# Clustered attention and two feed-forward layers: the first head pair's clusters chosen head by head, the second pair's preparation moved into the first ticks

## The chip, the cores and the metric

One core of a Trainium2 chip runs one program. Its engines work from queues of their own: TensorE (PE, with its weight loads shown as PEld), VectorE (DVE), ScalarE (ACT), GpSimd (POOL) and SyncE (SP), which only issues transfers here. The metric is the device time of one execution in microseconds, as the median of several runs. Lower is better.

## What is computed

Sixteen attention problems (2 batches by 8 heads, 768 tokens, 64 dimensions each) in which a query sees only the keys of its own cluster, then two feed-forward layers over all 1536 tokens:

```
q_assign = argmax(einsum('bhsd,hcd->bhsc', q_n, c_n))      # 16 clusters a head; q_n, k_n, c_n normalised
k_assign = argmax(einsum('bhsd,hcd->bhsc', k_n, c_n))
scores = where(q_assign[..., None] == k_assign[..., None, :], scale * q @ k.T, -1e9)
attn = softmax(scores) @ v
h = x @ w_in;  g = max(h, 0) + alpha * min(h, 0);  y = g @ w_out        # layer 1
h = y @ w_in2; g = max(h, 0) + log1p(exp(-abs(h))); out = g @ w_out2    # layer 2
```

Every product is done in split precision: an operand is stored as a high part (rounded to fp32r) and a low part (the rest), and the products of the parts are summed.

## The kernel before, in words

Attention goes by pairs of heads, eight pairs in all (`pairs`). The work on one pair is cut into named steps (`steps_of`). For its preparation they are, by name and line: `hik`/`hiq` high parts on ACT (L369, L372), `lok` low part of the keys on POOL (L383), `lq` low part of the queries on DVE (L388, two halves), `sq` squares (on ACT for the first two pairs, L329, on POOL for the others, L331), `fold` six halving additions of the squares on POOL (L348), `inv0` to `inv2` the inverse norms (Ln and Exp on ACT L131/L132, then `inv1`: a reciprocal on DVE L135 and two POOL additions, then `inv2`: a POOL scaling L139 and the reciprocal `rinv` on DVE L140), `dk`/`dq`/`dh`/`dl` the products with the centroids on PE (L403, tile `dps`), `de` their copies on ACT (L411), `dt` their transposes on PE (L428).

Choosing a cluster is then: `dn` = `dt` times `rinv` (DVE L442), `mx` its maximum over 16 clusters, `eq` comparison with the maximum and multiplication with a falling `rank`, `m2` the maximum again, and `oh` the one-hot row. For the first pair all six operations are on DVE and work on both heads, queries and keys at once (128x384 elements, L442 to L476), and `dn` stands in PSUM, in one of the two buffers that later hold scores. For other pairs some are on POOL, and `dn` stands in SBUF. The one-hot rows are transposed on PE (`ot`, L492) and become the mask rows: `rq` (ACT, L507) and `rk` (DVE, L511) write those of the first head straight into its operands `mq` and `mk`; `mr` (ACT, L500) writes a copy from which `mk1` sends the second head's by DMA.

The attention itself runs in 96 ticks, one for 128 queries of one head, 12 to a pair. In tick u stand, in this order: `scores(u)` (PE, four matmuls, tile `s`, L599/L600; two buffers), `exps(u-1)` (ACT L614, tile `e`), `maxima(u)` (DVE, tile `nm`, L605), steps due at phase E, `transposes(u-2)` (PE, tile `pt`, L627), `highs`/`lows` (ACT `ph` L643, DVE `pl` L647), `attend(u-4)` (PE, tile `o`), and steps due at phase L. The whole attention is under a manual schedule: each engine executes in the order in which the code is run, and stands still where its next instruction has to wait.

What is run before tick 0 is the list `PRELUDE`. Later steps stand in tables (`FIRST`, `SECOND`, `THIRD`, `STEADY`, `LAST`): a number x of pair n means tick (n-2)*12 + ceil(x), phase L for a whole number, else E. So in `SECOND` 12 is tick 0 and 15.5 is tick 4, phase E; in `FIRST` 24 is tick 0; in `THIRD` 3 is tick 3. `warm(n)` is n transposes of the identity on PE whose result (`wps`) nobody reads.

Before the change, `PRELUDE` holds also the second pair's squares, folds and low parts (`sq0 1`, `fold0 1`, `lq0 1`), and the second pair's `dn` and `mx` stand at 13.5 and 14, that is in tick 2.

## Time and profile before

| what | value |
|---|---|
| time, median of 3 runs | 807.17 us (806.46 to 807.91) |
| the profiled execution: span from first to last instruction | 804.5 us |
| what lies around that span in a run, by the difference | 2.7 us |
| busy share of the span: PE, DVE, ACT, POOL | 97%, 73%, 62%, 44% |
| mean granted TensorE clock, as a share of 2.4 GHz | 0.987 |
| first maximum of scores (`nm` of tick 0) starts at | 21.72 us |
| `nm` of tick 2, 5, 6 starts at | 28.60, 35.90, 39.55 us |

The opening is some 45 of 804.5 us. A microsecond in it counts in full where PE stays busy from there on. Times in rows are microseconds from the span's start.

### The profile page before, as it was taken

The page shows a single profiled execution, that of the slowest core. Times are in us where ns is not written, and L with a number is a line of the kernel's source. Part 1 is how long each engine was busy: PE and PEld are TensorE (multiplying, and loading weights), DVE is VectorE, ACT ScalarE, POOL GpSimd, SP SyncE. Part 2 cuts the span into 40 slices and gives each one's busy share as a digit, 9 for nine tenths or more (in the row PEclk, how much of TensorE's full clock was granted, in tenths as well). Part 3 has the DMA queues.
Part 4 walks back from the last instruction along what each step waited for, and adds up shares of the span by engine and source line. Part 5 has one row for each costly group of instructions (what it writes and reads, how often), then busy time and mean ns, then how long its engine had stood idle before and what let it go on. Part 6 is the DMA issues. An engine that isn't in the chain of part 4 may idle for free.

```text
span 804.5 us, 11964 instructions
## 1 busy us (share of the span) xinstructions
PE 780.4 (97%) x4139; PEld 666.7 (83%) x4139; DVE 585.3 (73%) x923; ACT 496.0 (62%) x1024; POOL 356.8 (44%) x380
## 2 busy tenths in 40 slices
PE   6899999999998979999999999999999999999998
PEld 6789999999997758888888888888888888888886
DVE  7689989989989977547646835978469569765444
ACT  5788999999999778346536535674366245343221
POOL 6567668778354775026115404585144036023000
PEclk9899999999999989999999999999999999999999
DMA  9666667655552343102302401312014012000002
GB/s 265 180 166 172 152 170 173 182 145 128 119 144 64 105 157 132 53 26 79 105 0 72 138 1 53 132 53 78 1 53 156 2 53 81 24 2 1 28 31 97
DMA packets 26955, 75.91 MB, mean 94 GB/s; under 512 B 4464, under 2 KB 7408, under 8 KB 26896
## 3 DMA queue, kind: packets, MB, share of 16 engines
q1 hardware_dynamic: 26896, 75.16, 32.3%
q8 instruction: 32, 0.52, 0.3%
q14 instruction: 27, 0.22, 0.1%
HBM read 49.36 MB, written 3.15 MB: 65 GB/s over the span
## 4 chain that ended last, share of the span: by engine, by line
PE 78%; DVE 11%; ACT 3%; POOL 3%; issue 3%; DMA 1%; SPq 0%; DVEq 0%; POOLq 0%; ACTq 0%
PE acc L935 29%; PE hp L876 27%; PE pt L627 6%; PE o L657 6%; PE s L599 3%; PE s L600 3%; DVE r L173 2%; DVE pl L647 2%; POOL t L178 1%; DVE nm L605 1%; PE dps L403 1%; DVE m L168 1%; DVE y L950 1%; DVE lo L388 1%; ACT e L614 1%
## 5 line engine op out<-in xcount | busy, mean ns | idle before, releaser
L876 PE MATMUL hp<-xh,ih 128*128 128x512 f32 x384 | 150.2, 392 | 1.3 <-ACT e L614 1.3
L876 PE MATMUL hp<-xl,ih 128*128 128x512 f32 x384 | 150.1, 391 | 0.0
L876 PE MATMUL hp<-xh,il 128*128 128x512 f32 x384 | 149.9, 391 | 0.0
L181 POOL TENSOR_TENSOR il<-t,ih 128x512 fp32r<-128x512 f32 x32 | 44.3, 1385 | 198.7 <-ACT ih L180 188.3
L917 DVE TENSOR_TENSOR gl<-hp,gh 128x512 fp32r<-128x512 f32 x96 | 65.9, 686 | 69.6 <-ACT gh L916 69.5
L916 ACT CAST gh<-hp 128x512 fp32r<-128x512 f32 x96 | 56.4, 587 | 88.8 <-PE acc L935 69.9
L605 DVE TENSOR_REDUCE nm<-s 128x1 f32<-128x768 f32 x96 | 90.9, 947 | 18.3 <-PE s L600 18.3
L647 DVE TENSOR_TENSOR pl<-pt,ph 128x384 fp32r<-128x384 f32 x192 | 97.3, 548 | 5.8 <-ACT ph L643 4.9
L178 POOL TENSOR_TENSOR t<-m,r 128x512 uint32<-128x512 uint32 x64 | 85.6, 1337 | 30.8 <-DVE r L173 16.3
L643 ACT CAST ph<-pt 128x384 fp32r<-128x384 f32 x192 | 84.0, 485 | 14.7 <-PE pt L627 14.1
L614 ACT ACTIVATE e<-s,nm 128x768 f32<-128x768 f32 x96 | 87.9, 916 | 3.0 <-DVE nm L605 2.4
L898 ACT ACTIVATE sp<-a 128x512 f32<-128x512 f32 x48 | 30.4, 632 | 92.5 <-DVE a L894 92.5
L627 PE MATMUL pt<-ident,e 128*128 128x128 f32 x576 | 83.2, 277 | 4.1 <-DVE pl L647 4.0
L876 PEld LDWEIGHTS hp<-xh,ih 128*128 128x128 f32 x384 | 72.4, 189 | 16.5 <-ACT e L614 1.6
L876 PEld LDWEIGHTS hp<-xh,il 128*128 128x128 f32 x384 | 72.5, 189 | 15.2
L876 PEld LDWEIGHTS hp<-xl,ih 128*128 128x128 f32 x384 | 72.4, 189 | 15.1
L627 PEld LDWEIGHTS pt<-ident,e 128*128 128x128 f32 x576 | 66.9, 141 | 16.4 <-DVE pl L647 13.0
L935 PE MATMUL acc<-gh,oh 128*128 128x512 f32 x192 | 72.6, 395 | 5.4 <-ACT gh L916 5.4
L935 PE MATMUL acc<-gl,oh 128*128 128x512 f32 x192 | 75.7, 394 | 0.2 <-DVE gl L917 0.2
L935 PE MATMUL acc<-gh,ol 128*128 128x512 f32 x192 | 75.2, 392 | 0.0
L935 PE MATMUL acc<-ol,gh 128*128 128x512 f32 x192 | 74.7, 389 | 0.0
L935 PE MATMUL acc<-oh,gh 128*128 128x512 f32 x192 | 74.7, 389 | 0.0
(171 smaller groups left out, 1671.8 us busy)
## 6 DMA issues: line engine op xcount, KB each, us to landing
raw<-in_w_in_dram SPq DMA_DIRECT2D x32, 512.0 KB, 3.3
raw<-in_w_out_dram SPq DMA_DIRECT2D x32, 512.0 KB, 3.3
tok<-in_qk_tok_dram SPq DMA_DIRECT2D x8, 768.0 KB, 6.1
ak<-hi SPq DMA_DIRECT2D x31, 192.0 KB, 3.0
...
```

The source lines that it names most:

```text
L178: nc.gpsimd.tensor_tensor(out=t.bitcast(U32), in0=mu, in1=r, op=ALU.add)
L181: nc.gpsimd.tensor_tensor(out=low, in0=t, in1=high.bitcast(F32), op=ALU.subtract)
L605: nc.vector.tensor_reduce(out=nm, in_=st[u]["s"][:, :, 0:HS], axis=AX.XY, op=ALU.max, negate=True)
L614: nc.scalar.activation(out=e.rearrange("p (a j) c -> p a (j c)", a=2), in_=st[u]["s"][:, :, 0:HS], func=AF.Exp, bias=st[u]["nm"], scale=1. ...
L627: nc.tensor.transpose(pt[:, j * P : (j + 1) * P], st[u]["e"][:, 3 * a + j, :], ident)
L643: nc.scalar.copy(out=dh, in_=src)
L647: nc.vector.tensor_tensor(out=dl, in0=src, in1=dh.bitcast(F32), op=ALU.subtract)
L657: nc.tensor.matmul(acc[key][:, 0:QG], lhsT=vv[:, j, 2 * hh : 2 * hh + 2, :].rearrange("p a d -> p (a d)"), rhs=grp[key][part][:, j, :], st ...
L876: nc.tensor.matmul(hp, lhsT=a_[:, cs], rhs=b_[:, c, ts], start=n == 0, stop=n == 3 * NC_ - 1)
L916: nc.scalar.copy(out=gh, in_=hp)
L917: nc.vector.tensor_tensor(out=gl, in0=hp, in1=gh.bitcast(F32), op=ALU.subtract)
L935: nc.tensor.matmul(accs[c], lhsT=a_, rhs=b_, start=opens and n == 0, stop=closes and n == 2)
```

## The change

The six operations of the choice become a function `choose(hh, parts)` that works on one head (128x192 elements, every other group of 16), and a pair's two heads are chosen apart:

```
+                    q["oh"] = ap1.tile([P, J, 4 * C], F32R, tag="oh", name="oh")
+                    nc.gpsimd.memset(q["oh"].bitcast(F32).rearrange("p j (s h c) -> p j s h c", s=2, h=2)[:, :, :, 1], 0.0)
+                    return
...
+            def choose(hh, parts):
+                one = [P, n_ // 2, C]
+                dn, mx, m2 = q["dn"][:, hh::2], q["mx"][:, hh::2], q["m2"][:, hh::2]
+                oh = q["oh"].rearrange("p j (n c) -> p (j n) c", c=C)[:, hh::2]
+                r_ = rank[:, None, :].to_broadcast(one)
+                if 0 in parts:
+                    nc.vector.tensor_tensor(
+                        out=dn,
+                        in0=q["dt"][:, 0 : n_ * C].rearrange("p (n c) -> p n c", c=C)[:, hh::2],
+                        in1=q["rinv"][:, hh::2, None].to_broadcast(one),
+                        op=ALU.mult,
+                    )
+                if 1 in parts:
+                    nc.vector.tensor_reduce(out=mx, in_=dn, axis=AX.X, op=ALU.max)
+                if 2 in parts:
+                    nc.vector.tensor_tensor(out=dn, in0=dn, in1=mx[:, :, None].to_broadcast(one), op=ALU.is_equal)
+                if 3 in parts:
+                    nc.vector.tensor_tensor(out=dn, in0=dn, in1=r_, op=ALU.mult)
+                if 4 in parts:
+                    nc.vector.tensor_reduce(out=m2, in_=dn, axis=AX.X, op=ALU.max)
+                if 5 in parts:
+                    nc.vector.tensor_tensor(out=oh, in0=dn, in1=m2[:, :, None].to_broadcast(one), op=ALU.is_equal)
...
-            def onehot(t):
-                if first_:
+            def onehot(t, near=False):
+                if near:
                     q["ot", t] = ps_t.tile([P, 512], F32R, tag="t", name="ot")
...
+                st_[f"on{t}"] = lambda t=t: onehot(t, True)
...
 PRELUDE = [
-    "hik0 0", "hik1 0", "lok 0", "hiq0 0", "hiq1 0", "warm 18", "centroids_high", "centroids_low", "lq0 0",
+    "hik0 0", "hik1 0", "lok 0", "centroids_high", "centroids_low", "hiq0 0", "hiq1 0", "warm 8", "lq0 0",
...
+    "lok 1", "hiq0 1", "hiq1 1", "warm 17", "dn 0", "ch0 0", "on0 0", "on1 0",
+    "dh0 1", "dh1 1", "op1a 0", "op1b 0", "op1c 0", "minus_alpha",
+    "rq0 0", "rk0 0", "rk1 0", "rq1 0", "ch10 0", "ch11 0", "go 0", "ld 1", "lt 1",
...
 FIRST = dict(
-    va0=24, va1=26, lv=26.5,
+    ch12=23.5, ch13=23.5, ch14=24, ch15=24, on0=25, on1=25, mr0=25, mr1=25.5, mk1=25.5, va0=24, va1=27, lv=27.5,
```

`ch0` is the first head's whole choice; `ch10` to `ch15` are the six operations of the second head's. The second head's one-hot columns are first set to zero by POOL, since the transposes `on0`/`on1` of the prelude read both heads' columns. They are run a second time in tick 1, when the second head is chosen. In `SECOND` the second pair's `sq0=12, sq1=12, lq0=12.5, lq1=13, fold0=13, fold1=13.5, fold2=14` are new, and `inv0` moves from 12 to 14, `inv1` from 12.5 to 15, `inv2` from 13 to 15.5, `dt` from 13 to 14, `dn` from 13.5 to 15.5, `mx` from 14 to 16, `eq` from 16 to 17, `m2` from 18 to 18.5. The warming transposes are 18, 8, 9 and 17 ahead of tick 0 (before: 18, 18 and 14).

What stands on DVE between the first pair's one-hot row and the seventh maximum, before (from tick 0 to tick 4; `mk` is `rk`, `nm` a maximum, `lo` is `lq`, the second and later `dn` and `mx` are the second pair's):

```order
L388 SCALAR_TENSOR_TENSOR lo<-dim,hi 128x384 x2
L511 TENSOR_SCALAR mk<-ot,mscale,mbias_96 16x384 x2
L605 TENSOR_REDUCE nm<-s 128x1 x2
L135 RECIPROCAL s_383<-s_367 128x24
L140 RECIPROCAL rinv<-s_383 128x24
L605 TENSOR_REDUCE nm<-s 128x1
L442 TENSOR_TENSOR dn<-dt,rinv 128x384
L647 TENSOR_TENSOR pl<-pt,ph 128x3x128 x2
L454 TENSOR_REDUCE mx<-dn 128x24
L605 TENSOR_REDUCE nm<-s 128x1
L647 TENSOR_TENSOR pl<-pt,ph 128x3x128 x2
L605 TENSOR_REDUCE nm<-s 128x1
```

The same place after the change, from the second maximum on (ahead of it stand the two `mk`, two operations of the second head's choice, the first `nm` and the other four):

```order
L626 TENSOR_REDUCE nm<-s 128x1
L387 SCALAR_TENSOR_TENSOR lo<-dim,hi 128x384 x2
L626 TENSOR_REDUCE nm<-s 128x1
L668 TENSOR_TENSOR pl<-pt,ph 128x3x128 x2
L626 TENSOR_REDUCE nm<-s 128x1
L668 TENSOR_TENSOR pl<-pt,ph 128x3x128 x2
L134 RECIPROCAL s_471<-s_436 128x24
L626 TENSOR_REDUCE nm<-s 128x1
L139 RECIPROCAL rinv<-s_471 128x24
L445 TENSOR_TENSOR dn<-dt,rinv 128x384
L668 TENSOR_TENSOR pl<-pt,ph 128x3x128 x2
L485 TENSOR_REDUCE mx<-dn 128x24
```

The two `lo` moved from ahead of the mask rows to between the maxima of ticks 1 and 2, and the two reciprocals, `dn` and `mx` of the second pair moved from ticks 1 and 2 to ticks 3 and 4, ahead of that tick's `pl`.

PE at the start of the ticks, before (rows from the first pair's one-hot transposes to the third unit's scores, with the queues whose signal each waits for):

```order
L492 MATMUL ot<-identr,oh 64x128 [waits DVE_49,PE_49]
L492 MATMUL ot<-identr,oh 64x128 x2
L492 MATMUL ot<-identr,oh 64x128 [waits PE_49]
L492 MATMUL ot<-identr,oh 64x128 x2
L599 MATMUL s<-ak,aq 128x384 [waits DMAHW1_49,DMAHW2_49,DMAHW0_49,Pool_49]
L600 MATMUL s<-mk,mq 128x384 [waits DVE_49,Pool_49]
L599 MATMUL s<-ak,aq 128x384
L600 MATMUL s<-mk,mq 128x384
L403 MATMUL dps<-lo,chz 64x384 [waits Pool_49]
L403 MATMUL dps<-lo,chz 64x384 x3
```

and after, from the same transposes on:

```order
L512 MATMUL ot<-identr,oh 64x128 [waits DVE_49,PE_49,Pool_49]
L512 MATMUL ot<-identr,oh 64x128 x2
L512 MATMUL ot<-identr,oh 64x128 [waits DVE_49]
L512 MATMUL ot<-identr,oh 64x128 x2
L402 MATMUL dps<-hi,chz 64x384
```

and, from the second unit's scores (ahead of them stand eight `dps<-hi` and the first unit's four) to the eight warming transposes:

```order
L620 MATMUL s<-ak,aq 128x384 [waits Activation_49]
L621 MATMUL s<-mk,mq 128x384
L620 MATMUL s<-ak,aq 128x384
L621 MATMUL s<-mk,mq 128x384
L512 MATMUL ot<-identr,oh 64x128 [waits DVE_49]
L512 MATMUL ot<-identr,oh 64x128 x5
L402 MATMUL dps<-lo,chz 64x384
L402 MATMUL dps<-lo,chz 64x384 [waits DVE_49]
L402 MATMUL dps<-lo,chz 64x384
L402 MATMUL dps<-lo,chz 64x384 [waits DVE_49]
L211 MATMUL wps<-ident 128x128 [waits Activation_49]
L211 MATMUL wps<-ident 128x128 x7
```

The second half's first transposes now wait for DVE: `dt` still holds one of the two buffers that they turn in, so both halves use the other, and `rk0` must have read the first. The second unit's scores wait for ACT: `dn` still holds one of the two buffers of the scores, so the first unit's `exps` must have read the other. The four `dps<-lo` products, the eight `wps` and the third unit's scores stand behind the two `lo` of DVE.

POOL in ticks 2 to 4, before:

```order
L565 TENSOR_TENSOR vv<-rawv,vv 128x6x64
L136 TENSOR_TENSOR s_383<-sq,s_383 128x24
L137 TENSOR_TENSOR s_383<-s_383,s_367 128x24
L139 TENSOR_SCALAR s_383<-s_383 128x24
L564 CAST vv<-rawv 128x6x64
```

and after:

```order
L586 TENSOR_TENSOR vv<-rawv,vv 128x6x64
L135 TENSOR_TENSOR s_471<-sq,s_471 128x24
L136 TENSOR_TENSOR s_471<-s_471,s_436 128x24
L330 TENSOR_TENSOR sq<-tok 128x768
L138 TENSOR_SCALAR s_471<-s_471 128x24
L486 TENSOR_TENSOR dn<-dn,mx 128x384
L382 TENSOR_TENSOR lo<-dim,hi 128x768
```

The third pair's squares (`sq<-tok`, `THIRD` has them in tick 3) now stand between the second and the third of the operations that make the second pair's inverse norm.

## Rows read from the trace of the kernel before

**Rows 1.** The page's first part: busy time and share of each engine.

```profile
PE 780.4 (97%) x4139; PEld 666.7 (83%) x4139; DVE 585.3 (73%) x923; ACT 496.0 (62%) x1024; POOL 356.8 (44%) x380
```

**Rows 2.** Three windows: length, then each engine's busy time (count), granted clock, DMA.

```profile
22.00:28.00 6.00, 5.55 (x24) 4.83 (x23) 2.24 (x4) 3.28 (x9) 3.00 (x6) 0.50 0.59 170
...
30.00:45.00 15.00, 13.08 (x89) 11.25 (x89) 13.06 (x23) 12.44 (x30) 8.75 (x7) 1.00 0.88 214
45.00:55.00 10.00, 10.00 (x83) 9.65 (x82) 8.12 (x13) 8.95 (x22) 6.85 (x11) 1.00 0.56 126
```

**Rows 3.** Timeline to 17 us: start, length, engine, line, tile, [idle before <-releaser].

```profile
7.75 1.58 ACT L329 ACTIVATE sq<-tok 128x768 f32<-128x768 f32 x2 [0.84 <-DMA tok<-in_qk_tok_dram]
...
12.69 0.57 DVE L442 TENSOR_TENSOR dn<-dt,rinv 128x384 f32<-128x384 f32 x1
...
13.69 1.82 POOL L383 TENSOR_TENSOR lo<-dim,hi 128x768 fp32r<-128x768 f32 x1 [4.06 <-ACT hi L369]
...
15.22 0.42 PE L403 MATMUL dps<-hi,chz 128*64 128x384 f32 x1
...
15.68 0.56 DVE L476 TENSOR_TENSOR oh<-dn,m 128x384 fp32r<-128x384 f32 x1
```

**Rows 4.** Groups to 60 us, shapes apart: total busy, mean ns, idle before.

```profile
L276 POOL MEMSET clz<- 128x384 f32 x1 | 0.4, 432 | 0.0
...
L261 DVE TENSOR_TENSOR csq<-cexp 128x128 f32<-128x128 f32 x1 | 0.3, 293 | 0.6 <-DMA cexp<-in_centroids_dram 0.6
```

**Rows 5.** Timeline 15.9 to 25 us: from the first one-hot row to the second maximum.

```profile
15.95 3.98 POOL L348 TENSOR_TENSOR sq<-sq 128x768 f32<-128x768 f32 x3 [0.43 <-ACT sq L329]
...
16.16 3.32 DVE L388 SCALAR_TENSOR_TENSOR lo<-dim,hi 128x384 fp32r<-128x384 f32 x2
...
16.70 0.53 PE L492 MATMUL ot<-identr,oh 128*64 128x128 f32 x6
...
17.08 0.66 ACT L507 ACTIVATE mq<-ot,mbias,mscale 16x384 fp32r<-16x384 f32 x1 [1.21 <-PE ot L492]
...
19.51 1.26 DVE L511 TENSOR_SCALAR mk<-ot,mscale,mbias 16x384 fp32r<-16x384 f32 x2
...
20.92 0.41 PE L600 MATMUL s<-mk,mq 80*128 80x384 f32 x1 [3.47 <-DVE mk L511]
...
21.72 0.96 DVE L605 TENSOR_REDUCE nm<-s 128x1 f32<-128x768 f32 x1 [0.94 <-PE s L600]
...
22.71 0.90 ACT L614 ACTIVATE e<-s,nm 128x768 f32<-128x768 f32 x1
...
24.07 0.96 DVE L605 TENSOR_REDUCE nm<-s 128x1 f32<-128x768 f32 x1 [1.40 <-PE s L600]
```

**Rows 6.** Timeline 25 to 42 us: ticks 2 to 6 (maxima of ticks 2, 5, 6).

```profile
25.32 1.97 PE L212 MATMUL wps<-ident 128*128 128x128 f32 x8
...
26.93 0.67 PE L599 MATMUL s<-ak,aq 128*128 128x384 f32 x1
...
28.60 0.96 DVE L605 TENSOR_REDUCE nm<-s 128x1 f32<-128x768 f32 x1 [1.97 <-PE s L600]
...
35.13 0.85 DVE L465 SCALAR_TENSOR_TENSOR dn<-dn,rank 128x384 f32<-128x384 f32 x1
...
35.90 0.94 DVE L605 TENSOR_REDUCE nm<-s 128x1 f32<-128x768 f32 x1
...
37.70 0.54 DVE L388 SCALAR_TENSOR_TENSOR lo<-dim,hi 128x384 fp32r<-128x384 f32 x1
...
39.55 0.96 DVE L605 TENSOR_REDUCE nm<-s 128x1 f32<-128x768 f32 x1 [1.31 <-PE s L600]
```

**Rows 7.** Timeline at 58 us: the third pair's inverse norm.

```profile
58.20 0.30 DVE L140 RECIPROCAL rinv<-s 128x24 f32<-128x24 f32 x1 [1.50 <-POOL s L139]
```

**Rows 8.** Groups to 60 us, shapes apart: POOL squares and ACT Ln.

```profile
L331 POOL TENSOR_TENSOR sq<-tok 128x768 f32<-128x768 f32 x3 | 4.7, 1569 | 0.1
...
L131 ACT ACTIVATE s<-sq,tiny 128x24 f32<-128x24 f32 x2 | 0.7, 338 | 0.0
```

More of the change, by code (lines that the diff above doesn't have):

```diff
@@ L447, in _ @@
                 )
+            def choose(hh, parts):
[20 more added lines that the diff above has]
+                    nc.vector.tensor_tensor(out=oh, in0=dn, in1=m2[:, :, None].to_broadcast(one), op=ALU.is_equal)
+            for hh in range(2):
+                for part in range(6):
+                    st_[f"ch{hh}{part}"] = lambda hh=hh, part=part: choose(hh, [part])
+                st_[f"ch{hh}"] = lambda hh=hh: choose(hh, range(6))
             @step("mx")
@@ L454, in _ @@
                 nc.vector.tensor_reduce(out=q["mx"], in_=dn, axis=AX.X, op=ALU.max)
-                if not first_:
-                    nc.gpsimd.tensor_tensor(out=dn, in0=dn, in1=q["mx"][:, :, None].to_broadcast(every), op=ALU.subtract)
+                nc.gpsimd.tensor_tensor(out=dn, in0=dn, in1=q["mx"][:, :, None].to_broadcast(every), op=ALU.subtract)
             @step("eq")
@@ L460, in _ @@
                 dn, r_ = q["dn"], rank[:, None, :].to_broadcast(every)
-                if first_:
-                    nc.vector.tensor_tensor(out=dn, in0=dn, in1=q["mx"][:, :, None].to_broadcast(every), op=ALU.is_equal)
-                    nc.vector.tensor_tensor(out=dn, in0=dn, in1=r_, op=ALU.mult)
-                else:
-                    nc.vector.scalar_tensor_tensor(
-                        out=dn, in0=dn, scalar=0.0, in1=r_, op0=ALU.is_equal, op1=ALU.mult
-                    )
+                nc.vector.scalar_tensor_tensor(
+                    out=dn, in0=dn, scalar=0.0, in1=r_, op0=ALU.is_equal, op1=ALU.mult
+                )
             @step("m2")
```

18 lines of the change are left out of this document (6 added, 12 removed), and 6 rows, old and new, of the table PRELUDE.

## The prediction

> **What bounds the kernel now.** Read first the shares by engine: PE is busy 97% of the span [rows 1], so outside the opening the time is PE's, and what the opening loses or gains is carried to the end. Then the windows. From 22 to 28 us PE's granted clock is 0.50, the lower of its two levels (1.2 GHz), and from 30 to 45 us it is 1.00, but DVE is busy 13.06 of 15 us and PE is not full [rows 2]: here DVE is the engine that sets the ticks. From 45 to 55 us PE is busy without a gap [rows 2]. Then the timeline. The first one-hot row is done at 16.24 (15.68 + 0.56) [rows 3], but DVE next runs the second pair's two `lo` for 3.32 us, until 19.48, and only then the mask rows `mk` for 1.26 us; PE stands 3.47 us for them, and the first maximum starts at 21.72, the second at 24.07 [rows 5]. The third waits for PE until 28.60: eight warming transposes of 0.2 us (25.32 to 26.93) and four products stand ahead of it. The maxima of ticks 5 and 6 are at 35.90 and 39.55 [rows 6].
>
> The change takes the two `lo` out of the first wait and halves the choice. It also puts new waits in, and DVE work into ticks that DVE sets. I walk through it, with the start of `nm` in each tick as the mark, in us against before.
>
> **1. Choice and memset (to the first transposes): -1.0.** The six operations stand 0.60 apart (12.69 to 15.68 is five of them) [rows 3]. Half width lies between 0.29 for 128 elements [rows 4] and 0.57 for 384 [rows 3], on a line 0.36, so 0.39 apart: six take 2.3. They begin where they did, since the squares wait for their load at 7.75 [rows 3], which nothing moves; at best 0.3 sooner, as the centroid copy goes ahead; I take 0.2. So DVE is done at 14.8. But the transposes read both heads' columns and wait for POOL's memset, behind POOL's `lo`, which ends at 15.51 [rows 3]. Half of a memset that took 0.43 [rows 4] is 0.25, so 15.5 to 15.7. On PE stand 17 warming transposes from 12.4; at 0.2 each [rows 6] they end at 15.8, less if the clock rises. I take 15.7 instead of 16.70 [rows 5].
>
> **2. Mask rows and first scores: -0.75 more.** From transposes to `rq` was 0.38, `rq` 0.66, each `mk` 0.63 [rows 5]. Before, the second half's transposes followed at once. Now they wait for `rk0`, and `rk0` for `rq0` (one buffer of PSUM serves both halves): `rq0` 16.1 to 16.75, `rk0` to 17.4, second transposes 17.5, `rk1` 17.9 to 18.5. PE has the eight `dps<-hi` behind those transposes; eight took 1.48 (15.22 to 16.70) [rows 3, 5]; they end at 19.2, and the four products of the first unit take 0.8 (three took 20.92 to 21.72 [rows 5]). `nm` of tick 0 starts at 20.0 instead of 21.72: -1.75. The second head's first two operations (0.8) fit on DVE while it waits.
>
> **3. Second unit's scores wait for the first unit's exponentials: +1.2, leaving -0.55.** `dn` keeps one of the two score buffers until the second head is chosen, so the second unit turns in the other. `nm` 0.96 and `e` 0.90 [rows 5] put its start at 21.95; before, it started right behind the first unit. Its four products take 1.5 at the lower clock level (four from 26.93 to 28.60 took 1.65 [rows 6]). `nm` of tick 1 at 23.5 instead of 24.07. The second head's other four operations (1.6) lie beside this.
>
> **4. The two `lo` between tick 1 and tick 2: +1.75, now +1.2.** They start at 24.5. One took 0.54 alone [rows 6] and 1.66 beside POOL's folds [rows 5]. POOL's folds now wait for the squares on ACT (1.58 [rows 3]), which follow `rq1` (done at 19.2), so they begin at 20.8; the first three alone took 3.98 [rows 5], and then come the values: POOL is busy beside both `lo`, with shorter instructions. I take 1.1 each, both ends kept. `lo` ends at 26.7, its product at 27.0, the eight warming transposes at 28.6, the third unit's scores (1.65 at the lower level, 0.8 at the higher; 1.2 taken) at 29.8. `nm` of tick 2 at 29.8 instead of 28.60.
>
> **A rule beside this step.** The Trainium skill, "GPSIMD Engine Reference", Key points, says that GpSimd shares its SBUF interfaces with VectorE and contends with VectorE instructions that have two SBUF inputs. `lo` has two, the choice with `dn` in PSUM has not, and the trace agrees: 1.66 beside folds, 0.57 for the choice beside POOL's `lo` [rows 3, 5]. By the rule alone both `lo` would be paid at 1.66, and the sum below would be 1.1 more.
>
> **5. Ticks 2 to 4: 0, stays +1.2.** `dn` and `mx` (0.57 and 0.56) leave DVE here; one reciprocal (0.30 [rows 7]) comes, and on ACT Ln and Exp (0.34 [rows 8] and about as much) now stand between `ph` and the third `e`, whose result DVE needs for its `pl`. Between -0.8 (only DVE counts) and +0.4 (only ACT counts); I take 0.
>
> **6. Tick 4, the inverse norm: +1.95, now +3.15.** `rinv` waits on DVE for POOL's chain, and `dn`, then both `pl`, `mx` and the next `nm` are queued behind it; PE's transposes wait for `pl`. In that chain now stand the third pair's squares, 1.57 [rows 8]. With two small additions (0.25 each) and the scaling (0.2) it is 2.3 to 2.4 after the reciprocal, of which one `nm` (0.96) covers the first part: a stall of 1.4. The same pattern is in the trace: at 58.20 DVE stood 1.50 for that scaling, with two POOL operations put between [rows 7]. It could be 0 (if `nm` is late for another reason) to 1.5. Then `rinv` 0.30, `dn` and `mx` 1.1; and the comparison with `rank` (0.85 [rows 6]) moves out of this tick: 1.4 + 1.4 - 0.85.
>
> **7. Tick 5: +0.85, now +4.0.** The comparison stands in tick 5 between `pl` and the third pair's `lo`, for which PE waits before it can make tick 6's scores; that `nm` had waited 1.31 for PE [rows 6], so nothing covers it. POOL's low part of the third pair's keys waits too, behind a subtraction that needs the late `mx`.
>
> **8. Tick 7: +0.5, now +4.5.** `m2` (0.56) stood where DVE waited for PE, and stands now ahead of the next `lo`, for whose product PE waits.
>
> **What costs nothing.** The loads of the third pair go ahead of the second head's mask rows in SP's queue; those rows are needed in tick 6, which was at 39.55 [rows 6]. The second head's transposes and rows run in ticks 1 and 2 beside the waits of steps 3 and 4; without them they would cost 0.5. From tick 8 on PE sets the ticks (45 to 55 us [rows 2]), and nothing there is bound to a fixed time, so no slack gives the 4.5 back.
>
> Sum: 804.5 + 4.5 = 809.0 for the span. The median of the runs lies 2.7 above the profiled span, so 811.7 us.
>
> **The rivals.**
>
> *The clock stays at its higher level.* PE fell to 0.50 after standing still [rows 2, 5], and the change spreads its products and warming transposes differently. If it does not fall, the second unit's scores save 0.75, the warming transposes 0.8, the third unit's scores 0.4: 809.8; with both `lo` at 0.54 also 808.7. For it: the long stand of 3.47 is gone. Against: waits of 1.5 to 2 us remain in steps 2, 3 and 4, and the last ended at the lower level before.
>
> *Not slower: DVE's added work in ticks 2 to 7 is hidden.* One mechanism: if PE and ACT set those ticks, steps 5 to 8 cost nothing and only step 4's mark counts: +1.2, or with `lo` at 0.54 about +0.1, so 807.3; with the clock up too, 805.3. It decides where `rinv` is ready when tick 4's `nm` ends. For it: 1.9 us of 15 are idle on DVE [rows 2]. Against: 1.31 of these are one wait, ahead of tick 6, and `lo` itself causes it [rows 6].
>
> *Worse.* The clock falls before the eight `dps<-hi`: they and the first unit's scores take double, +1.5; with `lo` at 1.66 each the sum is 814.3.
>
> **How the numbers follow.** I give the walk 0.50, the clock rival 0.24, the hidden work 0.21 (half of it faster, half the same), the worse case 0.05. A difference of 0.2%, 1.6 us, is about what a measurement can tell from no change. Slower by more: 0.78 (all of the walk and the worse case, most of the clock rival), within 0.11, faster 0.11. The predicted time is the walk's, 811.7. The range takes the clock rival and the upper half of the hidden work in, and upwards part of the worse case: 807.6 to 813.6.
>
> **What would show it.** Right: first `nm` at about 20.0, second near 23.5, third after 29; DVE idle over 1 us before the second pair's `rinv`, put down to POOL; `nm` of tick 6 at 43 to 45; everything from tick 8 on as before but 4 to 5 us later. Wrong: `lo` near 0.54 and the third `nm` before 28; no wait ahead of `rinv`; or a granted clock of 1.00 from 16 to 30 us.

## The result, and the profile after the change

The changed kernel took 814.94 us in the median of four runs (811.43 to 816.09), the kernel before 807.26 (806.46 to 807.91): a ratio of 1.0088, interval 1.0065 to 1.0110. Five more runs gave 814.41 beside 807.10, 1.0099 (1.0082 to 1.0117). It is slower, as forecast, but by 7.3 to 7.7 us and not by 4.5.

Two executions were traced: the first took 811.43 us, the lowest time of all, the second (run `again`) 814.40. The marks of the forecast, starts of `nm` in us:

| tick | before | forecast | first trace | second trace |
|---|---|---|---|---|
| 0 | 21.72 | 20.0 | 21.41 | 21.11 |
| 1 | 24.07 | 23.5 | 24.50 | 24.15 |
| 2 | 28.60 | 29.8 | 29.10 | 30.26 |
| 4 | 33.12 | 34.3 | 33.20 | 34.37 |
| 5 | 35.90 | 39.05 | 37.88 | 39.04 |
| 6 | 39.55 | 43.55 | 44.12 | 45.92 |
| 7 | 42.17 | 46.2 | 46.71 | 50.47 |
| 8 | 45.01 | 49.5 | 49.78 | 53.54 |
| 95 | 260.05 | 264.55 | 264.72 | 268.66 |
| span | 804.5 | 809.0 | 809.7 | 812.6 |

From tick 8 to tick 95 the distance to the kernel before stays what it is (4.77 and 4.67 in the first trace, 8.53 and 8.61 in the second), and what follows tick 95 takes 543.9 to 545.0 us in all three. So in these two traces everything is decided before tick 8. They are two of nine runs; of the other seven, 814.1 to 816.1 us, only the time is known.

The shares by engine of the first trace hardly differ from [rows 1]:

```profile
PE 782.5 (97%) x4147; PEld 666.9 (82%) x4147; DVE 585.1 (72%) x929; ACT 496.0 (61%) x1024; POOL 357.2 (44%) x381
```

Windows of the first trace (length, then each engine's busy time and count, granted clock, DMA), to be laid beside [rows 2]:

```profile
22.00:28.00 6.00, 4.01 (x21) 3.20 (x22) 3.64 (x8) 3.94 (x8) 5.39 (x8) 0.72 0.49 196
30.00:45.00 15.00, 11.28 (x66) 8.87 (x65) 11.89 (x20) 9.91 (x25) 6.47 (x7) 0.89 0.65 148
45.00:55.00 10.00, 9.76 (x76) 9.17 (x76) 8.21 (x15) 8.38 (x20) 6.55 (x7) 1.00 0.53 140
```

and of the second trace:

```profile
40.00:45.00 5.00, 2.88 (x9) 1.55 (x8) 3.97 (x4) 1.79 (x5) 3.56 (x3) 0.50 0.62 116
45.00:50.00 5.00, 5.00 (x21) 4.71 (x21) 2.07 (x3) 1.97 (x5) 0.00 (x0) 0.50 0.88 246
```

From 30 to 45 us no engine is full any more: PE falls from 13.08 to 11.28 us busy, DVE from 13.06 to 11.89. They wait for one another. In the second trace the clock is at its lower level (1.2 GHz, 0.50) from 40 to 50 us.

The opening in the timeline of the first trace (start, length, engine, line, operation, [idle before <-releaser]), beside [rows 5, 6]:

```profile
15.23 0.25 POOL L442 MEMSET oh<- 128x192 f32 x1
...
15.53 0.37 PE L512 MATMUL ot<-identr,oh 128*64 128x128 f32 x3 [1.30 <-POOL oh L442]
...
17.68 0.52 PE L402 MATMUL dps<-hi,chz 128*64 128x384 f32 x1
...
19.92 0.52 PE L402 MATMUL dps<-hi,clz 128*64 128x384 f32 x1
...
21.41 0.96 DVE L626 TENSOR_REDUCE nm<-s 128x1 f32<-128x768 f32 x1 [2.02 <-PE s L621]
...
23.44 0.45 PE L620 MATMUL s<-ak,aq 128*128 128x384 f32 x1 [2.07 <-ACT e L635]
...
25.38 1.05 DVE L387 SCALAR_TENSOR_TENSOR lo<-dim,hi 128x384 fp32r<-128x384 f32 x2
```

and its ticks 4 to 6, beside [rows 6, 7]:

```profile
33.88 1.47 POOL L330 TENSOR_TENSOR sq<-tok 128x768 f32<-128x768 f32 x1
...
35.67 0.30 DVE L139 RECIPROCAL rinv<-s 128x24 f32<-128x24 f32 x1 [1.58 <-POOL s L138]
...
38.84 1.82 POOL L382 TENSOR_TENSOR lo<-dim,hi 128x768 fp32r<-128x768 f32 x1
39.67 1.41 DVE L491 SCALAR_TENSOR_TENSOR dn<-dn,rank 128x384 f32<-128x384 f32 x1
40.62 1.78 POOL L330 TENSOR_TENSOR sq<-tok 128x768 f32<-128x768 f32 x1
41.00 1.82 DVE L387 SCALAR_TENSOR_TENSOR lo<-dim,hi 128x384 fp32r<-128x384 f32 x1
42.87 0.39 PE L402 MATMUL dps<-lo,chz 128*64 128x384 f32 x1 [1.16 <-DVE lo L387]
...
44.12 0.96 DVE L626 TENSOR_REDUCE nm<-s 128x1 f32<-128x768 f32 x1 [1.30 <-PE s L621]
```

The stall of 1.58 us ahead of `rinv`, behind POOL's squares, is the one that step 6 described. The times that follow are in no step of the prediction: the comparison with `rank` takes 1.41 us (0.85 before) and the third pair's `lo` 1.82 (0.54 before). Each runs beside one POOL instruction and ends 0.42 us after that one does (39.67 + 1.41 = 41.08 and 38.84 + 1.82 = 40.66; 42.82 and 42.40). PE waits for POOL's low part and then for DVE's, and only then makes tick 6's scores.

The second trace at the same places:

```profile
8.85 1.58 ACT L328 ACTIVATE sq<-tok 128x768 f32<-128x768 f32 x2 [1.93 <-DMA tok<-in_qk_tok_dram]
...
25.02 2.07 DVE L387 SCALAR_TENSOR_TENSOR lo<-dim,hi 128x384 fp32r<-128x384 f32 x2
...
42.16 1.81 DVE L387 SCALAR_TENSOR_TENSOR lo<-dim,hi 128x384 fp32r<-128x384 f32 x1
...
44.41 0.52 PE L620 MATMUL s<-ak,aq 128*128 128x384 f32 x1
...
46.82 1.63 PE L678 MATMUL o<-ph,vv 128*128 128x256 f32 x6
...
50.47 0.96 DVE L626 TENSOR_REDUCE nm<-s 128x1 f32<-128x768 f32 x1 [2.19 <-PE s L621]
```

The same long `lo`, and then PE's products at 0.52 instead of 0.34 us until 50 us: tick 7 comes 4.55 us after tick 6, where it was 2.59 in the first trace. The first pair's squares also start 1.1 us later (8.85; 7.74 in the first trace), since their load landed later.

### The profile page after: what moved, and what is told of

Same layout as the page of the kernel before. It is cut to its first block, busy times and chain, and to the rows that moved or that the text cites. A ratio compares the mean times of both kernels' runs of the same rounds, so it can differ in the third digit from the quotient of the medians.

```text
span 809.7 us, 11982 instructions
## 1 busy us (share of the span) xinstructions
PE 782.5 (97%) x4147; PEld 666.9 (82%) x4147; DVE 585.1 (72%) x929; ACT 496.0 (61%) x1024; POOL 357.2 (44%) x381
## 4 chain that ended last, share of the span: by engine, by line
PE 76%; DVE 9%; POOL 5%; issue 4%; DMA 2%; ACT 2%; SPq 0%; POOLq 0%; DVEq 0%; ACTq 0%
PE acc L956 29%; PE hp L897 27%; PE pt L648 6%; PE o L678 6%; PE s L620 3%; PE s L621 3%; DVE r L172 2%; DVE m L167 1%; DVE pl L668 1%; DMA tok<-in_qk_tok_dram 1%; POOL t L177 1%; POOL sq L347 1%; PE dps L402 1%; DVE nm L626 1%; DVE y L971 1%
## 5 line engine op out<-in xcount | busy, mean ns | idle before, releaser
L897 PEld LDWEIGHTS hp<-xh,ih 128*128 128x128 f32 x384 | 72.2, 188 | 15.7 <-ACT xh L773 0.8
```

Source lines behind the costliest of these rows:

```text
L897: nc.tensor.matmul(hp, lhsT=a_[:, cs], rhs=b_[:, c, ts], start=n == 0, stop=n == 3 * NC_ - 1)
```

## The experiments

Fourteen more kernels were timed (`again` is the changed kernel itself), in four groups, and the kernel before beside each group; its median moved by up to 0.7 us from group to group (806.41 to 807.10), so medians of different groups can be compared to within about that. The interval belongs to the ratio.

| label | base and edit | median us | before, beside it | ratio (interval) |
|---|---|---|---|---|
| again | changed kernel | 814.41 | 807.10 | 1.0099 (1.0082 to 1.0117) |
| e_sq | changed, third pair's squares later | 812.07 | 807.10 | 1.0073 (1.0054 to 1.0091) |
| e_quiet | changed, those squares earlier | 811.49 | 806.41 | 1.0056 (1.0037 to 1.0075) |
| e_dots | changed, PE's use of `lo` later | 812.25 | 807.00 | 1.0067 (1.0049 to 1.0086) |
| e_clock | changed, PE kept busy | 814.65 | 806.41 | 1.0099 (1.0079 to 1.0118) |
| e_dn | changed, first `dn` in SBUF | 817.33 | 807.10 | 1.0130 (1.0111 to 1.0150) |
| e_late | before + late inverse norm | 811.66 | 807.07 | 1.0050 (1.0032 to 1.0067) |
| e_ab | changed - late inverse norm | 811.00 | 807.07 | 1.0050 (1.0033 to 1.0068) |
| e_rows | before + mask rows ahead | 807.62 | 807.10 | 1.0020 (1.0005 to 1.0036) |
| b_va | before, values a tick later | 804.65 | 806.41 | 0.9974 (0.9963 to 0.9986) |
| e_mend | e_quiet and b_va | 808.98 | 807.07 | 1.0024 (1.0011 to 1.0036) |
| best1 | e_rows, b_va, squares earlier | 807.09 | 806.41 | 0.9997 (0.9984 to 1.0011) |
| b_now | b_va without eight `warm` | 805.84 | 807.07 | 0.9986 (0.9974 to 0.9999) |
| best2 | b_va, folds behind the low parts | 804.89 | 807.00 | 0.9982 (0.9969 to 0.9996) |

**again.** No edit. 

> The changed kernel itself, unaltered, as the control for the runs beside it and as a second trace of it. The profiled execution of the changed kernel took 811.43 us, the other three 814.8 to 816.1, so 3.3 to 4.7 us are in no trace yet. Theory A (the opening's clock differs from execution to execution): if a longer execution is caught, the maxima of ticks 2 to 8 start 3 to 4 us later than in the first trace (tick 8 at 53 instead of 49.78), with more time at the lower granted clock between 15 and 45 us. Theory B (the end differs): tick 8 is at 49.8 as before and the difference lies after 290 us or later in the feed-forward part, with a lower granted clock there. If a short execution is caught: 811 to 812 and nothing is told apart. Median against before: +6 to +8 us.

A longer execution was caught, and theory A holds: tick 8 is 3.76 us later than in the first trace, while what follows it is 0.8 us shorter. It is not the opening alone, though: 1.16 us are there by tick 2, and 2.6 come in ticks 5 to 7.

**e_sq.**

```
-THIRD = dict(STEADY, hik0=3, sq0=3, ...
+THIRD = dict(STEADY, hik0=3, sq0=4.5, ...
```

> The changed kernel with the first squares of the third pair one tick and a half later, so that they no longer stand on POOL between the additions and the scaling of the second pair's inverse norm. Theory (that stall of 1.58 us and what it makes late sets ticks 5 and 6): the wait ahead of rinv falls to 0 to 0.3, the maximum of tick 5 starts at 36.2 to 36.6 instead of 37.88, that of tick 6 at 41.5 to 43 instead of 44.12, and the time falls by 1.3 to 2.5 us against the control. Rival 1 (the stall only moves: the squares now stand ahead of the third pair's later products, or POOL runs beside the low parts): tick 5 is earlier by 1.4 but tick 6 by less than 0.5, time within 0.6 of the control. Rival 2 (the granted clock is the cause): no tick moves by more than 0.5 and time is the control's.

The wait ahead of `rinv` fell to 0.15 us. Tick 5 came 7.63 us after tick 2 (8.78 in both traces of the changed kernel): the stall was paid, at 1.15. Tick 6 came another 6.25 us later, as before the edit (6.24 in the first trace): the squares still run beside `lo`, which took 1.82 again. The time fell by 2.3, inside the theory's range, but the marks did not come where it had them (tick 5 at 37.38, tick 6 at 43.63), since tick 2 itself came at 29.75, and tick 6 moved little, as rival 1 had it. The trace's own share is 1.15; the rest of the 2.3 was not located.

**e_quiet.**

```
-THIRD = dict(STEADY, hik0=3, sq0=3, hik1=3, hiq0=4, lok=4, hiq1=5, sq1=5, ...
+THIRD = dict(STEADY, hik0=3, sq0=2.5, hik1=3, hiq0=4, lok=4, hiq1=5, sq1=2.5, ...
-  q["sq"] = ap1.tile([P, n_, D], F32, tag="sq", name="sq")
+  q["sq"] = ap1.tile([P, n_, D], F32, tag="sq", name="sq", bufs=2)
```

> The changed kernel with the third pair's squares in a second buffer and on POOL in ticks 2 and 3, where POOL stands idle, so that neither they stand in the chain of the second pair's inverse norm, nor do they run beside VectorE's low part in tick 5. In the kernel that moved them the other way, behind POOL's low part (e_sq), tick 5 came 7.63 us after tick 2 and tick 6 another 6.25 us later; the comparison with rank took 1.41 us beside POOL's low part and the low part 1.81 us beside the squares. Theory (contention between POOL and VectorE is the larger part of what tick 5 costs): the low part falls to 0.5 to 0.7 us, the comparison stays at 1.4, tick 6 comes 4.7 to 5.3 us after tick 5, the clock has less reason to fall, and the time is 1.2 to 2.5 us under that of e_sq (812.07), 809.6 to 810.9. Rival (PE's wait for POOL's own low part sets tick 6, whatever VectorE's takes): tick 6 comes 6.0 us or more after tick 5, time as e_sq's.

Timeline of this kernel, tick 5:

```profile
39.11 1.81 POOL L382 TENSOR_TENSOR lo<-dim,hi 128x768 fp32r<-128x768 f32 x1
...
39.94 1.40 DVE L491 SCALAR_TENSOR_TENSOR dn<-dn,rank 128x384 f32<-128x384 f32 x1
41.26 0.55 DVE L387 SCALAR_TENSOR_TENSOR lo<-dim,hi 128x384 fp32r<-128x384 f32 x1
...
43.11 0.96 DVE L626 TENSOR_REDUCE nm<-s 128x1 f32<-128x768 f32 x1 [1.30 <-PE s L621]
```

With POOL idle `lo` takes 0.55; the comparison, still beside POOL's low part, keeps its 1.40. Tick 6 comes 4.97 us after tick 5 instead of 6.24 to 6.88: the contention theory holds, the rival falls. The median, 811.49, missed the forecast of 809.6 to 810.9: ticks 14 to 17 took 9.00 us (7.12 before), at a granted clock of 0.83 from 60 to 70 us, behind the stall of tick 13 [rows 7]. The same 1.9 us are lost at the same place in the traces of e_dots, e_ab and e_rows (9.00 and 9.01), and not in those of the kernel before and the changed kernel (7.12 and 7.13), which have the same stall.

**e_dots.**

```
-THIRD = dict(STEADY, ..., lt=5.5, lq0=5, dk0=5, fold0=7)
+THIRD = dict(STEADY, ..., lt=5.5, lq0=5, dk0=6, dq0=6, de0=6.5, dk1=7, fold0=7)
```

> The changed kernel with PE's products of the third pair's distances one tick later (their operands are made when they were), so that in tick 5 no product that needs a low part stands ahead of the scores of unit 6. Theory A (PE's wait for the two low parts is what tick 5 costs, and the last stand after which the clock falls): tick 6 comes 4.7 to 5.3 us after tick 5, set by VectorE's own chain (nm 0.87, pl 0.93, comparison 1.33, low part 1.8), instead of 6.24 to 6.88, tick 7 2.6 to 3.3 us after that, and the median falls from 814.4 to 810.5 to 813. Theory B (the waiting only moves into tick 6, where the same products stand ahead of unit 7's scores): tick 6 earlier by 1.3, tick 7 by less than 0.5, median 814 or more.

Timeline of this kernel:

```profile
45.23 1.82 DVE L387 SCALAR_TENSOR_TENSOR lo<-dim,hi 128x384 fp32r<-128x384 f32 x1
46.97 0.94 DVE L626 TENSOR_REDUCE nm<-s 128x1 f32<-128x768 f32 x1
...
47.10 0.39 PE L402 MATMUL dps<-lo,chz 128*64 128x384 f32 x1 [0.94 <-DVE lo L387]
```

Theory A: tick 6 came 4.88 us after tick 5, with no wait for PE ahead of it, although `lo` still took 1.82; tick 8 came 9.84 us after tick 5 (11.90 and 14.50 in the two traces), and the clock stayed at 1.00 from 40 to 50 us. The median fell by 2.2 against that of `again`. The traced execution was the longest of these runs (814.65): its clock was 0.50 from 15 to 30 us, and tick 2 came at 32.62.

**e_clock.**

```
+if u == 5 and c == 0:
+    for _ in range(10):
+        nc.tensor.matmul(s[:, c, 0:HS], lhsT=aq[:, qs], rhs=ak[:, ks], start=True, stop=True)
...
+if n == 2 and t == 0 and (s_, m) == (1, 0):
+    for _ in range(8):
+        nc.tensor.matmul(q["dps", t][0 : 2 * HC, 0:HS], lhsT=..., rhs=..., start=True, stop=True)
```

> The changed kernel with work added on PE alone, where PE waits: the first score product of unit 5 is computed eleven times instead of once, and the first product of the third pair's distances nine times (the extra ones are overwritten). Nothing else is altered. In the two traces of the changed kernel tick 7 came 2.59 and 4.55 us after tick 6, the latter with a granted clock of 0.50 from 40 to 45 us. Theory (PE's stand around 36 to 42 us lets the clock fall, and this is why some executions are 3 to 4 us longer): the clock stays at 1.00 from 38 to 50 us, tick 7 comes 2.6 us after tick 6 in the trace, and the median falls from the control's 814.4 to 810.5 to 812. Rival (the clock is not tied to that stand, or the extra products only push the scores later): median 814 or more, tick 7 as late as in the longer trace.

The rival is right about the time. Timeline of PE, tick 5 to 7:

```profile
45.77 0.39 PE L408 MATMUL dps<-lo,chz 128*64 128x384 f32 x1 [1.41 <-DVE lo L387]
45.99 0.51 PE L629 MATMUL s<-ak,aq 128*128 128x384 f32 x1
...
48.44 1.46 PE L687 MATMUL o<-ph,vv 128*128 128x256 f32 x6
```

From 35 to 45 us the clock held at 1.00, and then PE stood 1.41 us for `lo`, a wait that the extra products do not cover; the next products took 0.51, and tick 7 came 3.62 us after tick 6. So the long stand for `pl` (1.95 us in the first trace, 0.23 here) is not needed for a fall. What would become of the clock with the stand for `lo` filled as well, this run does not tell, and its time holds the extra products too.

**e_dn.**

```
-  s_ = ps_s.tile([P, 2, 512], F32, tag="s", name="dn")
-  q["dn"] = s_[:, 0, 0 : n_ * C].rearrange("p (n c) -> p n c", c=C)
+  q["dn"] = ap1.tile(every, F32, tag="dn", name="dn")
```

> The changed kernel with the first pair's scaled distances in SBUF, so that they hold no score buffer and the second unit's scores need not wait for the exponentials of the first. Theory (this wait sets tick 1): the second unit's scores start right behind the first unit's, at 21.4 to 21.6 instead of 23.44, the maximum of tick 1 starts at 23.0 to 23.4 (behind nm of tick 0 and the second head's choice on DVE) instead of 24.50, tick 2 at 27.8 to 28.6 instead of 29.10, and tick 8 is 0.5 to 1.3 us earlier, as is the time. Rival (DVE is busy with the second head's choice anyway, or the choice gets slower beside POOL since both of its inputs are then in SBUF): tick 1 moves by less than 0.4 and the time by less than 0.4.

The second unit's scores did follow the first unit's directly (22.34), but tick 1 still came 3.11 us after tick 0 (3.09 and 3.04 with the wait), and the time rose by 2.9. Its timeline:

```profile
13.42 1.81 POOL L382 TENSOR_TENSOR lo<-dim,hi 128x768 fp32r<-128x768 f32 x1 [4.08 <-ACT hi L368]
...
13.59 1.85 DVE L469 TENSOR_TENSOR dn<-dn,rank 128x192 f32<-128x192 f32 x1
```

With `dn` in PSUM the same multiplication takes 0.37. With both inputs in SBUF it ends 0.21 after POOL's low part (15.44 and 15.23), and takes 1.05 for the second head, beside POOL's folds. So the run took one wait away and put another in: it doesn't price the wait for the exponentials. The traces of the changed kernel give a bound: ahead of tick 1's maximum DVE stood 0.61 and 0.55 us for PE, with the second head's choice done. As a whole, `dn` in PSUM is worth more here than the buffer that it holds.

**e_late.** The second pair's `sq`, `fold`, `inv`, `dn`, `mx`, `eq` and `m2` at the places of the change, all else as before:

```
-"sq0 1", "sq1 1", "fold0 1", "fold1 1", "fold2 1",                          (PRELUDE)
-inv0=12, inv1=12.5, inv2=13, dt=13, dn=13.5, mx=14, eq=16, m2=18            (SECOND)
+sq0=12, sq1=12, fold0=13, fold1=13.5, fold2=14, inv0=14, dt=14, inv1=15,
+inv2=15.5, dn=15.5, mx=16, eq=17, m2=18.5
```

> The kernel before with one part of the change alone: the second pair's squares, folds, inverse norm and what hangs on it (its scaled distances, maxima, comparison) go into ticks 0 to 7 as the change has them; choice, mask rows and low parts stay as before. Theory (this part costs the change its time): VectorE stands 1.4 to 1.6 us ahead of the second pair's rinv, tick 5 comes 8.5 us or more after tick 2 (7.30 before), tick 6 another 6 us or more after that (3.65 before), so the ticks from 8 on lose 3.5 to 4.5 us against tick 2; the low parts, no longer beside POOL's folds, fall from 1.66 to about 0.55 each, which starts tick 0 about 2 us earlier; in sum 809 to 812. Rival (the cost belongs to the new order of the opening, not to the late inverse norm): tick 6 within 1 us of before, time 805 to 808.

Theory. Timeline of this kernel:

```profile
16.32 1.02 DVE L388 SCALAR_TENSOR_TENSOR lo<-dim,hi 128x384 fp32r<-128x384 f32 x2
...
33.33 0.30 DVE L140 RECIPROCAL rinv<-s 128x24 f32<-128x24 f32 x1 [1.39 <-POOL s L139]
```

Without folds beside them both low parts take 1.02 us (3.32 in [rows 5]); tick 0 starts at 19.68, tick 2 at 23.51, 5.1 us earlier than before. All of it and 2.3 more is lost by tick 6 (41.80; 6.28 after tick 5). By tick 8 the loss against tick 2 is 7.6 us where 3.5 to 4.5 were expected; the time came inside the range since the gain ahead of tick 2 was larger too. A wait that the expectation did not have: ACT stood 2.97 us with Ln, at 27.78, for the late folds, and `ph` and `e` were queued behind it.

**e_ab.** The counterpart: the changed kernel with these steps back in the opening and in ticks 0 to 4.

```
-SECOND: sq0=12, sq1=12, fold0=13, fold1=13.5, fold2=14, inv0=14, inv1=15, inv2=15.5, dn=15.5, mx=16, eq=17, m2=18.5
+SECOND: inv0=12, inv1=12.5, inv2=13, dn=14.5, mx=15, eq=16, m2=18
+PRELUDE: "sq0 1", "sq1 1", "fold0 1", "fold1 1", "fold2 1" behind "dn 0"
```

> The changed kernel with that same part undone: the choice stays head by head and the mask rows ahead, but the second pair's squares and folds are back in the opening, and its inverse norm, scaled distances and comparison back in ticks 0 to 4 (half a tick later than before). Theory: no stall ahead of rinv in tick 4, tick 5 comes 7.0 to 7.8 us after tick 2 and tick 6 another 3.6 to 5.0 us later, and the time falls by 3 to 6 us against the control, to 808 to 811. Rival (the choice head by head, which starts tick 0 only 0.3 us earlier and tick 2 later than before, carries the loss): 812 or more.

No stall ahead of `rinv` in tick 4, tick 5 7.74 after tick 2, tick 6 4.89 after tick 5: as the theory had it, and the time fell by 3.4. Of the loss 3.9 us remain. In this trace they are not all the opening's: tick 8 is 2.3 us later than before (47.32 and 45.01), and 1.9 more are lost in ticks 14 to 17, at a clock of 0.83 from 60 to 70 us. So the late inverse norm is about half of the loss; of the other half the new order of the opening has 2.3 us in the trace.

**e_rows.**

```
-dl0=12, dl1=12, inv0=12, de0=12.5, de1=12.5, inv1=12.5, inv2=13, dt=13, dn=13.5, op0a=13.5, mx=14,
+inv0=12, lq0=12.5, lq1=12.5, inv1=12.5, inv2=13, dl0=13, dl1=13, de0=13, de1=13, dt=14, dn=14.5, op0a=13.5, mx=15,
```

(and `lq0 1`, `lq1 1` out of `PRELUDE`). 

> The kernel before with one part of the change alone: the first pair's mask rows go ahead of the second pair's two low parts, which move into tick 1. The choice stays joint, and the second pair's squares, folds, inverse norm and its scaled distances stay in the opening, the latter a half to one tick later. Theory (the late inverse norm and the displaced comparison of ticks 4 to 7 cost the change its 4.7 us, the mask rows ahead gain): the maximum of tick 0 starts at 19.3 to 20.5 instead of 21.72, that of tick 2 at 27.5 to 29, ticks 5 to 8 within 0.7 of before or up to 1.5 earlier, time 0 to 2 us under that of before. Rival (low parts in the ticks cost as much there as they gave ahead of them, or the clock falls where PE waits): tick 2 at 29 or later and time 0 to 2 us over that of before.

Neither text came out whole. Tick 0 started at 18.77, tick 2 at 26.28, tick 6 at 39.16, 0.4 earlier than before, so the theory's ticks came, or better; then ticks 14 to 17 took 9.01 us (7.12 before), at a clock of 0.83 from 60 to 70 us, and the trace ends 1.4 us later than before, the time that the rival had. With the joint choice tick 0 is 1.3 us earlier than head by head in e_ab (20.09).

**b_va.**

```
-mk0=21.5, va0=22, mk1=22.5, va1=24, lv=25, go=23,
+mk0=21.5, va0=22, mk1=22.5, va1=25, lv=25.5, go=23,
```

> The kernel before with one thing moved: POOL makes the second pair's second half of the values one tick later, so that they no longer stand between the additions and the scaling of the third pair's inverse norm, for which VectorE stood 1.50 us at 58.20 (tick 13). It prices the same pattern that the change puts into tick 4, at a place where nothing else is changed. Theory (such a stall is paid, since the maxima of both neighbouring ticks queue behind it): the stall falls below 0.3 us, tick 13 comes 2.7 us after tick 12 instead of 3.90, and all after it is 1.0 to 1.3 us earlier, 805.8 to 806.2. Rival (PE is busy there and sets the ticks): the stall goes but ticks 15 to 20 move by less than 0.3 us, time as before.

```profile
56.45 0.30 DVE L140 RECIPROCAL rinv<-s 128x24 f32<-128x24 f32 x1
56.67 0.89 DVE L605 TENSOR_REDUCE nm<-s 128x1 f32<-128x768 f32 x1
```

The stall of 1.50 is gone, tick 13 comes 2.36 us after tick 12 (3.90 before), and the median falls by 1.8, more than the 1.0 to 1.3 expected: such a stall is paid in full, and this version beats both kernels.

**e_mend.** The edits of e_quiet and b_va together. 

> The changed kernel with both mends that the runs point to: the third pair's squares early in a second buffer (as e_quiet, 811.49) and the second pair's second half of the values one tick later (as b_va). In the trace of e_quiet the stall of tick 13 was still there, and behind it ticks 14 to 17 took 9.00 us (7.12 before) at a granted clock of 0.91 from 60 to 80 us. Theory: tick 13 comes 2.4 us after tick 12 instead of 3.9, the clock does not fall behind it, and the time is 1.5 to 3 us under that of e_quiet, 808.5 to 810; still above the kernel before. Rival (no effect beyond the tick's own): 810.5 or more.

Tick 13 came 2.36 after tick 12, ticks 14 to 17 took 7.13 us, and the median is 2.5 under that of e_quiet, as the theory had it. In this trace, though, the clock fell earlier: PE stood 1.55 us for POOL's low part in tick 5, as in e_quiet, the granted clock was 0.50 from 42 to 44 us, and tick 7 came 4.17 us after tick 6 (2.59 in e_quiet). It remains some 4 us over b_va.

**best1.** e_rows and b_va, and `sq0=2`, `sq1=2` in `THIRD`. 

> The kernel before with its mask rows ahead of the second pair's low parts (as e_rows: choice still joint, squares, folds and inverse norm still in the opening), the third pair's squares on POOL in tick 2, where POOL stood idle for 6.25 us, and the second pair's second half of the values one tick later (as b_va). In e_rows PE waited 1.03 us for POOL's low part of the third pair and 1.11 us for VectorE's (1.80 us beside the squares), and tick 6 came 4.90 us after tick 5. Theory (contention and POOL's order): that low part falls to about 0.6, tick 6 comes 3.2 to 3.7 us after tick 5, at 37.3 to 38.0 us, tick 13 another 1.2 us earlier, and the time is 2 to 4 us under that of before where the clock does not fall, 803 to 805. Rival (what is gained shortens nothing, since the clock falls at the new waits): 806 to 808, with a granted clock below 0.95 somewhere between 45 and 100 us.

Tick 6 came 3.66 us after tick 5, as the theory had it, but tick 5 only 0.1 earlier than before (35.82). Tick 2, at 27.00, was still 1.6 us early; ticks 2 to 5 then took 8.82 us (7.30 before), with the second pair's `dn` and `mx` now in tick 3 and the comparison at 1.42 us (0.85 before) beside POOL's low part. The time is neither better nor worse than before. That is the rival's time and not its reason: in this trace the clock stayed at 1.00 from 45 to 100 us.

**b_now.** b_va without `at(1)(lambda: warm(8))`. 

> The kernel with the values one tick later (b_va, 804.65), without the eight warming transposes that PE runs in tick 1, ahead of the third unit's scores (25.32 to 26.93 in the kernel before, at the lower granted clock). Theory (they stand on the path and buy nothing): the maximum of tick 2 starts 1.0 to 1.6 us earlier, at 26.8 to 27.4, and the time falls to 803.2 to 804. Rival (without them the clock comes back later): the products of ticks 2 to 4 take 0.5 instead of 0.34 us, what is gained in tick 2 is gone by tick 5, time 804.5 or more.

The rival's time, but not by its reason. Tick 2 came at 26.67, 1.7 us earlier than in b_va, and tick 5 still 1.7 earlier (34.02): the clock was 1.00 in ticks 2 to 4. All of it was lost in tick 5, where `lo`, now beside POOL's squares, took 1.81 us (0.54 in b_va):

```profile
35.74 1.47 POOL L331 TENSOR_TENSOR sq<-tok 128x768 f32<-128x768 f32 x1
...
35.81 1.81 DVE L388 SCALAR_TENSOR_TENSOR lo<-dim,hi 128x384 fp32r<-128x384 f32 x1
```

PE stood 1.11 us until 37.67, its products took 0.52 from 38.05 on, and tick 6 came at 39.57, 0.2 later than in b_va. Of the 1.9 us lost in this tick 1.27 are `lo`'s: a change that left POOL's steps alone lost most of its gain by the same meeting.

**best2.**

```
-FIRST: va0=24, va1=26, lv=26.5          SECOND: inv0=12, inv1=12.5, inv2=13, dn=13.5, mx=14
+FIRST: va0=24, va1=30, lv=30.5          SECOND: fold0=12, fold1=12, fold2=12, inv0=14, inv1=14.5, inv2=15, dn=15, mx=15.5
-PRELUDE: "fold0 1", "fold1 1", "fold2 1",
```

> The kernel b_va (804.65) with POOL's folds of the second pair behind the first values, where they no longer run beside VectorE's two low parts ahead of the mask rows, and the inverse norm and what hangs on it in ticks 2 to 4; the first pair's second half of the values in tick 6. It tells whether the contention found in tick 5 is also what the two low parts of the opening cost. Theory (contention: 1.66 us each beside the folds, 0.51 in e_late without them): both low parts take 1.0 to 1.1 us together instead of 3.3, tick 0 starts at 19.4 to 19.9, tick 2 at 23.3 to 24.5, tick 6 at 35.5 to 38 instead of 39.35, and the time is 1 to 4 us under that of b_va. Rival (the late inverse norm, as in e_late, makes ACT or VectorE stand in ticks 3 to 5, or the clock falls there): tick 6 at 39 or later, time 804 or more.

The low parts took 1.02 together and tick 0 started at 19.55, as the theory had it; tick 2 came at 25.95 (23.3 to 24.5 expected), and by tick 6 (39.15) all was given back, as the rival had it. The place:

```profile
33.33 1.84 POOL L383 TENSOR_TENSOR lo<-dim,hi 128x768 fp32r<-128x768 f32 x1
33.41 2.18 DVE L465 SCALAR_TENSOR_TENSOR dn<-dn,rank 128x384 f32<-128x384 f32 x1
```

The comparison started 0.08 us after POOL's low part and ended 0.42 us after it did (35.59 and 35.17). The time is that of b_va within what can be measured.

## Why the prediction was right in its direction and wrong in its size

Step 1 was right: in the first trace the first transposes wait for POOL's memset and start at 15.53 (forecast 15.7). That nothing moves the first load was wrong for the second trace, where it landed 1.1 us later.

Step 2: the order was right, the clock not. In the first trace the eight `dps<-hi` stand 0.32 us apart (17.68 to 19.92 is seven of them), at the lower level, and tick 0 came at 21.41 instead of 20.0; so began the rival named *Worse*. In the second trace they ran at the higher level, and 21.11 less the 1.1 us of the late load is the forecast.

Step 3 was right about the wait (2.07 us behind `e`) and priced it too high: tick 1 came 3.09 and 3.04 us after tick 0, 2.35 before, so 0.7 and not 1.2. The second unit's products ran at the higher level (from 23.44 to 24.50, 1.06 us; 1.5 taken).

Step 4, forecast at +1.2 in tick 2, came out at +0.5 and +1.66. The two `lo` took 0.53 each in the first trace and 1.03 each in the second (1.1 taken). The two rows of the choice that the rule was held against, at 12.69 and 15.68, stand just outside POOL's `lo` (13.69 to 15.51); those between them, beside it, took 0.56 and 0.57 too.

Step 5: ticks 2 to 4 gave 0.4 back (4.10 and 4.11 us, 4.52 before), inside its bounds.

Step 6 was right: stall 1.58 and 1.57 (1.4 taken), tick 5 4.68 and 4.67 us after tick 4, 1.9 more than before (1.95 forecast). e_sq and e_quiet took the stall away and got 1.15 and 1.05 of tick 2 to 5 back; b_va priced the same pattern elsewhere at 1.54 (3.90 less 2.36).

**Step 7 is the step that failed.** It took the comparison at 0.85 and left the third pair's `lo` at 0.54, as in [rows 6]. Tick 6 was to come 4.50 us after tick 5, 0.85 more than before; it came 6.24 and 6.88 us after, 2.6 and 3.2 more. The late `mx` had moved POOL's subtraction, and with it POOL's low part and the second half of the squares, beside just these two DVE instructions, and each ran until 0.42 us behind POOL's: 0.56 and 1.28 us more (1.41 less 0.85, 1.82 less 0.54), which with the forecast 4.50 makes 6.34. e_quiet took POOL away from beside `lo` and got 1.27 back (6.24 to 4.97); e_dots took PE's wait away and got 1.36 (6.24 to 4.88). The prediction weighed just this contention in step 4, with both ends, and did not ask what POOL would be doing in step 7.

Nor was 0.85 the comparison's own time. Timeline of the kernel before, POOL beside the comparison of [rows 6]:

```profile
33.72 1.85 POOL L383 TENSOR_TENSOR lo<-dim,hi 128x768 fp32r<-128x768 f32 x1
```

and of e_quiet, where the next pair's comparison met no work of POOL:

```profile
75.56 0.54 DVE L491 SCALAR_TENSOR_TENSOR dn<-dn,rank 128x384 f32<-128x384 f32 x1
```

Alone it takes 0.54. Before the change it already met the end of POOL's low part (until 35.57) and ended 0.41 behind it, at 35.98. So the row that step 7 took its price from held this contention already; POOL's row shows it.

The Trainium skill has the mechanism: "SBUF — State Buffer", section "SBUF: two separate sides", says that a GpSimd instruction that reads SBUF and a VectorE instruction with two SBUF inputs share a pair of ports under an exclusive lock, held for a whole instruction. The traces agree in these places: DVE's instruction ends 0.42 us behind POOL's (128x384; twice in the first trace, in e_quiet, in best2) or 0.21 behind it (128x192, e_dn). In one place they don't, shown in the last section.

**No step held the second loss.** In both traces the clock fell ahead of tick 6, but in the second it stayed down until 50 us; that trace is 1.96 us longer than the first between ticks 6 and 7, and 0.64 between 5 and 6. With it the sum is +8.5 at tick 8, 4.0 over the forecast, of which step 7 has 2.4 and the time from tick 6 to 7 has 1.9. Without it, in the first trace, it is +4.8, near the forecast 4.5, and that is luck: step 4 came out 0.7 lower, ticks 2 to 4 gave 0.4 back, step 8 came out 0.3 lower, and step 7 came out 1.7 higher. The rival *The clock stays at its higher level* asked about the clock between 16 and 30 us alone, and no case had a fall of the clock between ticks 4 and 7, so the range ended at 813.6.

Step 8 was half its size (0.23; 3.07 against 2.84 us between ticks 7 and 8).

The rival *Not slower* is refuted: ticks 4 to 6 did not hide the work. The parts by themselves: late inverse norm +4.6 (e_late), choice and mask rows without it +3.9 (e_ab), mask rows alone +0.5 (e_rows). The first two add up to 8.5 and not to the 7.3 us of the whole, so the parts are not independent. By the medians the choice head by head, which with the mask rows was to gain 0.55 us in steps 1 to 3, costs some 3.4 us of e_ab's; by the marks of tick 8 (2.3 later than before in e_ab, 0.4 earlier in e_rows) 2.7. That is a difference of two experiments, not a run of its own.

It stays open which stand of PE is followed by a fall of the clock. In the changed kernel PE stood 1.95 and 1.96 us until 37.09 and 38.25, and less than 2 us later its products ran at the lower level in both traces; the higher one was back at 41 us in the one and at 50 in the other. In e_quiet PE stood 1.55 us for POOL in tick 5 and the clock stayed; behind the same stand of 1.55 it fell in e_mend, and in e_clock behind one of 1.41.
